# Decode attention over a 65536-row cache on one core: the programs of ACT, SP and GpSimd run the steady heads as loops

## The chip, the core and the metric

The kernel runs on one core of one Trainium2 chip. The core has a matrix engine (PE, with its weight loads shown as PEld), a vector engine (DVE), a scalar engine (ACT), GpSimd (POOL) and a synchronizing engine (SP) that here issues nearly all DMAs. Every engine runs a program of its own; the programs meet only at semaphores. Sixteen DMA engines carry data between HBM and the on-chip memory. The metric is device time in microseconds (us), as the median of several runs. Before the change it is 2518.57 us over three runs (2518.57 to 2519.21).

## The reference

One token of a decode step goes through two branches that a gate mixes: attention over a long cache and a small gated feed-forward.

```python
# x [1,1,512]; k_cache, v_cache [1,32,65536,128]; wq [512,4096]; wo [4096,512]
def _A_ref(x, k_cache, v_cache, wq, wo):
    B, Sq, D = x.shape
    H, Dh = 32, 128
    q = (lambda x, *d: x.transpose(*d))((x @ wq).reshape(B, Sq, H, Dh), 0, 2, 1, 3)
    scores = jnp.einsum("bhqd,bhkd->bhqk", q, k_cache) * (Dh ** -0.5)
    p = _softmax(scores, axis=-1)
    o = jnp.einsum("bhqk,bhkd->bhqd", p, v_cache)
    return (lambda x, *d: x.transpose(*d))(o, 0, 2, 1, 3).reshape(B, Sq, H * Dh) @ wo

def _B_ref(x, w_gate, w_up, w_down):   # 512 -> 1792 -> 512
    g = _silu(x @ w_gate)
    u = x @ w_up
    return (g * u) @ w_down

x = A_x
g = _sigmoid((x * gate_w).sum(-1, keepdims=True))
a = _A_ref(x, A_k_cache, A_v_cache, A_wq, A_wo)
b = _B_ref(x, B_w_gate, B_w_up, B_w_down)
return g * a + (1 - g) * b
```

Inputs are bf16. K and V of one head are 16.78 MB each, and both caches together 1073.7 MB, every byte of which is read once.

## The kernel before

A head's K (65536 rows of 128) is read in two halves of 8.39 MB, z = 0 and 1, and so is its V. A half lies in the on-chip memory as 128 partitions with 64 KB each, taken from 256 consecutive cache rows. The array `mem` is one pool in which these halves have fixed places: `KA` and `KZ` for the K halves, `VA` and `VZ` for the V halves; the places of V overlap those of K and of each other in part, which is why a load has to wait until particular pieces of the half before have been used. Weights and the tail of the last head use the same pool.

For every head DVE transposes K in 16 pieces, 8 of each half (`nc.vector.transpose`, lines 405 and 412; line 336 for head 0), each adding 1 to `ktdone`, into the two buffers of `kt`. PE multiplies each piece with the head's query `qcur` (line 462) and adds 1 to `qkdone`. After the 16th piece DVE takes the row maximum (line 350, `s_mx`). POOL takes the maximum over partitions (`partition_all_reduce`, line 280, `s_ar`), ACT scales it (line 305), computes the exponentials and their row sums in one activation (line 307, `expdone`) and copies the next head's query from `qd` to `qcur` (line 310, `s_qc`). POOL sums the row sums over partitions (line 282, `s_L`). DVE rearranges the exponentials into `pb` in two halves (line 345, `s_pba`, `s_pbz`). PE then multiplies them with V (line 515), four groups of matmuls a head, each of which adds 1 to `pvdone`; these run one head late, between the score matmuls of the next head. ACT normalizes the resulting row (`row_norm`, line 299, `s_or`), PE turns it into a column (line 489, `s_pt`) and ACT puts that column into `oTn` (line 301).

The order of work on each engine is written out by hand. PE runs the 32 heads in a hardware loop (`Fori`, line 494) with further loops inside it, and DVE runs heads 1 to 31 in one (line 393). The programs of SP, POOL and ACT are written out head by head by Python loops: SP at lines 226 to 238, POOL at 278 to 282, ACT at 303 to 312. In these the limits of waits and all addresses are constants, and a wait is carried by the instruction that follows it.

SP's order for one head h is: first K half of h, first V half of h - 1, second K half of h, second V half of h - 1. Each has a wait ahead of it: K waits on `ktdone` (pieces transposed out of the place that it overwrites), V on `pvdone` (value matmuls done). All go to one queue and are carried out in the order of issue. Head 1 has other limits than the rest. After the last head, SP loads the output weights `wo` and the last head's V in pieces of falling size (lines 239 to 250). PE ends with the sums over these pieces (line 544) and the projection (lines 559 and 583), ACT rounds the result (line 314), and SP and ACT store it.

Of the kernel before, what the change touches and what calls it, by code (L numbers as in the profile page):

```python
# [5 lines left out]
P = 128  # L6
# [9 lines left out]
ds = bass.DynSlice  # L16
# [5 lines left out]
def bass_gated_mix__mha_block_cached__swiglu_ffn__decode_kernel(  # L22
# [11 lines left out]
    out: bass.AP,  # L34
):
    _, H, S, Dh = A_k_cache.shape
    D = A_wq.shape[0]
    F = B_w_gate.shape[1]
# [4 lines left out]
    NP = HR // PR  # L43
# [5 lines left out]
    KA, KZ, VA, VZ, V0 = 32, 0, 120, 96, 96  # L49
# [15 lines left out]
    with ExitStack() as ctx:  # L65
        def sb(name, shape, dt):
            return ctx.enter_context(nc.sbuf_tensor(name, shape, dt))

        def psum(name, shape, dt):
            return ctx.enter_context(nc.psum_tensor(name, shape, dt))  # L70

        def sem(name):
            return ctx.enter_context(nc.semaphore(name))
# [6 lines left out]
        psT = psum("psT", [P, 512], F32)  # L80
# [5 lines left out]
        qd = sb("qd", [P, H, 4, 4], BF16)  # L86
        qcur = sb("qcur", [P, 4, 4], BF16)
# [8 lines left out]
        gcol = sb("gcol", [P, 2], F32)  # L96
# [5 lines left out]
        oTn = sb("oTn", [P, H], BF16)  # L102
# [6 lines left out]
        def at(kb, n):  # L109
            return mem[:, kb * KB:kb * KB + n]  # L110
# [9 lines left out]
        d = {n: sem("d_" + n) for n in names}  # L120
# [21 lines left out]
        s_qc = sem("s_qc")  # L142
# [3 lines left out]
        s_b = sem("s_b")  # L146
        s_dch = sem("s_dch")
        ktdone = sem("ktdone")
        qkdone = sem("qkdone")
        pvdone = sem("pvdone")  # L150
        s_mx = sem("s_mx")
        s_ar = sem("s_ar")
        s_nb = sem("s_nb")
        expdone = sem("expdone")
        s_pba = sem("s_pba")
# [5 lines left out]
        s_otn = sem("s_otn")  # L161
# [34 lines left out]

        def place(kind, h, z):
            if kind == "k":
                return (KA, V0)[z] if h == 0 else (KA, KZ)[z]
            return (VA, VZ)[z]  # L200

        def kv_dram(cache, h):
            return cache[0, h].rearrange("(b p r) d -> b p (r d)", b=2, p=P)

        for n, kb in (("wq", WQ), ("wg", WG), ("wu", WU), ("wd", WD)):
            src = w_dram[n]
# [7 lines left out]
        @block.sync  # L214
        def _(sp):
            def load(kind, h, z):
                cache = A_k_cache if kind == "k" else A_v_cache
                sp.dma_start(at(place(kind, h, z), HR * Dh), kv_dram(cache, h)[z]).then_inc(d[kind + "az"[z]], 16)

            half = HR // 2 * Dh  # L220
            for n in range(2):
                sp.dma_start(at(KA + 32 * n, half), kv_dram(A_k_cache, 0)[0][:, n * half:n * half + half]).then_inc(
                    (d["ka0"], d["ka"])[n], 16)
            sp.wait_ge(s_q, 1)
            load("k", 0, 1)
            for h in range(1, H):
                sp.wait_ge(ktdone, 2 * NP * h - 4 if h > 1 else NP)
                load("k", h, 0)
                if h == 1:
                    sp.wait_ge(ktdone, 2 * NP - 3)  # L230
                    sp.wait_ge(s_b, 1)
                else:
                    sp.wait_ge(pvdone, 4 * h - 1)
                load("v", h - 1, 0)
                sp.wait_ge(ktdone, 2 * NP * h + NP // 2)
                load("k", h, 1)
                sp.wait_ge(pvdone, 4 * h + 1)
                load("v", h - 1, 1)
            sp.wait_ge(ktdone, 2 * NP * H - NP)
            sp.dma_start(at(WO, 31 * D), w_dram["wo"][:, 0:31 * D]).then_inc(d["wo"], 16)  # L240
            src = A_v_cache[0, H - 1].rearrange("(b p r) d -> b p (r d)", b=2, p=P)
            need = {0: (ktdone, 2 * NP * H - 4), 1: (ktdone, 2 * NP * H), 2: (pvdone, 4 * H - 1)}
            for n, (kb, r0, nr) in enumerate(tail):
                if n in need:
                    sp.wait_ge(*need[n])
                b, o = divmod(r0, HR)
                sp.dma_start(at(kb, nr * Dh), src[b][:, o * Dh:(o + nr) * Dh]).then_inc(dt_[n], 16)  # L247
            sp.wait_ge(pvdone, 4 * H)
            sp.dma_start(at(WOJ, D), wj_dram).then_inc(d["wj"], 16)
            sp.dma_start(at(WO31, D), w31_dram).then_inc(d["w31"], 16)  # L250
            sp.wait_ge(s_fin, 1)
            sp.dma_start(out_dram[2:4, :], fin[32:34, :]).then_inc(s_out2, 16)

        @block.gpsimd
        def _(pool):
            nc.gpsimd.memset(onesf[0:1, :], 1.0)
            nc.gpsimd.memset(sel, 0.0).then_inc(s_sel0, 1)
            pool.wait_ge(s_sel0, 1)
            for je in range(4):
                off = 64 * (je // 2) + je % 2  # L260
                v = sel[:, je, :].rearrange("p (g d) -> p g d", g=4)
                last = nc.gpsimd.affine_select(out=v, in_=v, compare_op=ALU.not_equal, fill=1.0, base=-off,
                                               pattern=[[0, 4], [-2, 32]], channel_multiplier=1)
            last.then_inc(s_sel, 1)
            nc.gpsimd.memset(unit[:], 0.0).then_inc(s_unit0, 1)
            pool.wait_ge(s_unit0, 1)
            nc.gpsimd.affine_select(out=unit[:], in_=unit[:], compare_op=ALU.not_equal, fill=1.0, base=0,
                                    pattern=[[-1, 4]], channel_multiplier=1).then_inc(s_unit, 1)
            nc.gpsimd.memset(bmat[:], 0.0).then_inc(s_b0, 1)
            for q in range(4):  # L270
                pool.wait_ge(s_b0, q + 1)
                nc.gpsimd.affine_select(out=bmat[:], in_=bmat[:], compare_op=ALU.not_equal, fill=1.0, base=-32 * q,
                                        pattern=[[-1, 32]], channel_multiplier=1).then_inc(s_b0, 1)
            nc.gpsimd.memset(hot[0:1, :, :], 0.0).then_inc(s_hot0, 1)
            pool.wait_ge(s_hot0, 1)
            nc.gpsimd.affine_select(out=hot[0:1, :, :], in_=hot[0:1, :, :], compare_op=ALU.not_equal, fill=1.0,
                                    base=0, pattern=[[1, 2], [-1, 2]], channel_multiplier=0).then_inc(s_hot, 1)
            for h in range(H):
                pool.wait_ge(s_mx, h + 1)
                nc.gpsimd.partition_all_reduce(amx, mxs, P, RMAX).then_inc(s_ar, 1)  # L280
                pool.wait_ge(expdone, h + 1)
                nc.gpsimd.partition_all_reduce(Lt, rsum, P, RADD).then_inc(s_L, 1)  # L282

        @block.scalar
        def _(act):
            act.wait_ge(s_z, 1)
            nc.scalar.activation(sc[0:1, 1:2], sc[0:1, 0:1], ACT.Exp, scale=-1.0).then_inc(s_e1, 1)
            act.wait_ge(s_qd, 1)
            nc.scalar.copy(qcur[:], qd[:, 0, :, :]).then_inc(s_qc, 1)
            act.wait_ge(s_gp, 1)  # L290
            nc.scalar.copy(gcol[:], psM[:, 8:10]).then_inc(s_gc, 1)
            act.wait_ge(s_h, 1)
            nc.scalar.activation(hbuf[:, 0, 0:FC], psM[:, 64:64 + FC], ACT.Exp, scale=-1.0).then_inc(s_sig, 1)

            def row_norm(h):
                act.wait_ge(s_li, h + 1)
                act.wait_ge(pvdone, 4 * h + 8)
                act.wait_ge(s_pt, h + 1)
                nc.scalar.mul(orow[0:4, :], psO[0:4, :], Li[0:4, :]).then_inc(s_or, 1)  # L299
                act.wait_ge(s_pt, h + 2)  # L300
                nc.scalar.mul(oTn[:, h:h + 1], psT[:, 0:1], gcol[:, 0:1]).then_inc(s_otn, 1)  # L301

            for h in range(H):
                act.wait_ge(s_ar, h + 1)
                nc.scalar.mul(nbias, amx, -SCALE).then_inc(s_nb, 1)  # L305
                act.wait_ge(s_nb, h + 1)
                nc.scalar.activation(pa[:], psS[:], ACT.Exp, bias=nbias, scale=SCALE,  # L307
                                     accum_out=rsum).then_inc(expdone, 1)
                if h < H - 1:
                    nc.scalar.copy(qcur[:], qd[:, h + 1, :, :]).then_inc(s_qc, 1)  # L310
                if h >= 1:
                    row_norm(h - 1)
            act.wait_ge(s_z4, 1)
            nc.scalar.copy(fin[0:34, :], psZ[0:34, 0:128]).then_inc(s_fin, 1)  # L314
            act.wait_ge(s_fin, 1)
            act.dma_start(out_dram[0:2, :], fin[0:2, :]).then_inc(s_out, 16)
# [297 lines left out]
```

## Time and profile before

| what | value |
|---|---|
| median of three runs | 2518.57 us |
| the profiled execution, whole | 2518.66 us |
| its span | 2517.4 us |
| mean granted clock of PE | 0.711 of full speed |
| instructions in the trace | 50622 |
| read from HBM | 1087.77 MB, 432 GB/s over the span |
| busy: PE, DVE, ACT, POOL | 1675.3, 1397.7, 65.6, 26.8 us |

The span is the time from the first to the last instruction of the profiled execution; 1.26 us of that execution's time lie around it. The page of the profile cuts the span into 40 slices. A row of the form "SPq" is an instruction of the engine's own sequencer, such as the issue of a DMA, a branch or an operation on registers; such rows are not counted as busy time. A row of waits names the engine and line that waited, what ended the wait, the total, how many times, and the longest. The time from a DMA's issue to its landing includes the time that it spends behind earlier DMAs.

### The profile page before, as it was taken

Reading aid. Unit: us, or ns where it says so; the run is one execution under the profiler, and the core shown is the slowest. Engines: PE = TensorE matmul, PEld = TensorE weight load, DVE = VectorE, ACT = ScalarE, POOL = GpSimd, SP = SyncE. Lnnn points to the kernel's source line nnn. Section 1 sums busy time; section 2 is a strip of 40 time slices with the busy share of each in tenths; the row PEclk is TensorE's granted clock in tenths of the full one; section 3 lists DMA queues with packets and bytes.
Section 4 is the critical chain, followed back from the end, with each engine's and each line's share of the span. In section 5 each row is a group of like instructions: output and inputs, shape, how many; then the busy total and the mean of one; then the engine's idle time right before and its main releaser. Section 6 shows DMA issues by size and latency. Waiting matters only on the chain.

```text
span 2517.4 us, 50622 instructions
## 1 busy us (share of the span) xinstructions
PE 1675.3 (67%) x21432; PEld 956.8 (38%) x21432; DVE 1397.7 (56%) x1631; ACT 65.6 (3%) x195; POOL 26.8 (1%) x83
## 2 busy tenths in 40 slices
PE   4566756667666577566676666766657756667667
PEld 3333333333433334333333333343333433333334
DVE  3764565554655645646456555465464564644653
ACT  0000000000000000000000000000000000000000
POOL 0000000000000000000000000000000000000000
PEclk8667767677677677676776767767767767677677
DMA  9999999999999999999999999999999999999999
GB/s 418 433 433 434 435 433 433 434 433 433 433 433 433 433 433 433 433 433 433 433 435 432 434 433 434 433 434 433 434 433 433 433 433 434 433 433 433 433 434 396
DMA packets 20474, 1087.97 MB, mean 432 GB/s; under 512 B 2282, under 2 KB 2668, under 8 KB 2924
## 3 DMA queue, kind: packets, MB, share of 16 engines
q1 hardware_dynamic: 20452, 1087.78, 99.9%
q8 instruction: 9, 0.15, 0.0%
q14 instruction: 5, 0.04, 0.0%
q10 hardware_dynamic: 8, 0.00, 0.0%
HBM read 1087.77 MB, written 0.00 MB: 432 GB/s over the span
## 4 chain that ended last, share of the span: by engine, by line
DMA 72%; PE 27%; DVE 0%; issue 0%; SPq 0%; ACT 0%
DMA mem<-in_A_v_cache_dram 70%; PE psO L515 27%; DMA mem<-in_A_k_cache_dram 2%; DMA mem<-in_A_wq_dram 1%; DVE kt L336 0%; PE psM L446 0%; SPq L247 0%; PE psZ L583 0%; PE psW L544 0%; ACT fin L314 0%
## 5 line engine op out<-in xcount | busy, mean ns | idle before, releaser
L462 PE MATMUL psS<-qcur,kt 128*128 128x4 bf16 x16384 | 573.7, 169 | 776.4 <-DVE kt L405 458.4
L515 PE MATMUL psO<-mem,pb 128*4 128x512 bf16 x3968 | 1033.6, 428 | 35.2 <-DMA mem<-in_A_v_cache_dram 35.2
L405 DVE STREAM_TRANSPOSE kt<-mem 128x2048 uint32<-128x2048 uint32 x248 | 551.2, 2280 | 571.9 <-DMA mem<-in_A_k_cache_dram 571.0
L462 PEld LDWEIGHTS psS<-qcur,kt 128*128 128x128 bf16 x16384 | 534.7, 106 | 852.4 <-issue 850.0
L412 DVE STREAM_TRANSPOSE kt<-mem 128x2048 uint32<-128x2048 uint32 x248 | 547.6, 2274 | 407.6 <-DMA mem<-in_A_k_cache_dram 407.6
L515 PEld LDWEIGHTS psO<-mem,pb 128*4 128x4 bf16 x3968 | 361.2, 93 | 666.2 <-issue 235.7
L345 DVE COPY pb<-pa 32x64 bf16<-32x64 bf16 x1024 | 233.5, 228 | 24.2 <-PE psO L515 9.5
L350 DVE TENSOR_REDUCE sm<-psS 128x1 f32<-128x512 f32 x32 | 22.1, 692 | 42.3 <-PE psS L462 42.3
L336 DVE STREAM_TRANSPOSE kt<-mem 128x2048 uint32<-128x2048 uint32 x16 | 35.4, 2277 | 16.9 <-DMA mem<-in_A_k_cache_dram 16.9
L280 POOL PARTITION_ALL_REDUCE sm<-sm x32 | 11.2, 351 | 2392.6 <-DVE sm L350 2392.6
L301 ACT ACTIVATE oTn<-psT,gcol 128x1 bf16<-128x1 f32 x31 | 8.2, 263 | 1063.2 <-PE psT L489 1063.2
L489 PE MATMUL psT<-unit,orow 4*128 4x1 f32 x256 | 33.5, 248 | 0.8 <-ACT orow L299 0.8
L299 ACT ACTIVATE orow<-psO,sm 4x512 f32<-4x512 f32 x31 | 21.0, 677 | 439.5 <-issue 439.5
L489 PEld LDWEIGHTS psT<-unit,orow 4*128 4x128 f32 x256 | 30.8, 186 | 1.9 <-ACT orow L299 1.3
L305 ACT ACTIVATE sm<-sm 128x1 f32<-128x1 f32 x32 | 6.5, 203 | 886.3 <-POOL sm L280 886.3
L307 ACT ACTIVATE pa<-psS,sm 128x512 bf16<-128x512 f32 x32 | 22.0, 687 | 1.0
L544 PE MATMUL psW<-pb,mem 128*128 128x1 bf16 x512 | 14.6, 165 | 7.6 <-DMA mem<-in_A_v_cache_dram 7.1
L544 PEld LDWEIGHTS psW<-pb,mem 128*128 128x128 bf16 x512 | 14.1, 102 | 8.7 <-issue 6.5
L282 POOL PARTITION_ALL_REDUCE sm<-sm x32 | 12.3, 383 | 36.4 <-ACT pa L307 36.4
L446 PE MATMUL psM<-xTb,mem 128*128 128x1 bf16 x128 | 3.6, 165 | 11.1 <-DMA mem<-in_A_wq_dram 11.1
L474 PE MATMUL psM<-xTb,mem 128*128 128x1 bf16 x112 | 6.9, 198 | 4.9 <-DMA mem<-in_B_w_up_dram 4.9
L432 DVE TENSOR_SCALAR w<-psW,sm 128x2 bf16<-128x2 f32 x1 | 0.2, 221 | 16.5 <-PE psW L544 16.5
(64 smaller groups left out, 63.1 us busy)
## 6 DMA issues: line engine op xcount, KB each, us to landing
mem<-in_A_v_cache_dram SPq DMA_DIRECT2D x3, 4096.0 KB, 29.4
mem<-in_A_k_cache_dram SPq DMA_DIRECT2D x2, 4096.0 KB, 38.8
mem<-in_A_wq_dram SPq DMA_DIRECT2D x1, 4096.0 KB, 12.6
mem<-in_A_wo_dram SPq DMA_DIRECT2D x1, 3968.0 KB, 37.0
mem<-in_A_v_cache_dram SPq DMA_DIRECT2D x1, 2048.0 KB, 32.9
mem<-in_B_w_gate_dram SPq DMA_DIRECT2D x1, 1792.0 KB, 16.4
mem<-in_B_w_up_dram SPq DMA_DIRECT2D x1, 1792.0 KB, 21.3
mem<-in_B_w_down_dram SPq DMA_DIRECT2D x1, 1792.0 KB, 25.1
```

Of the source, the lines that this page charges most:

```text
L282: nc.gpsimd.partition_all_reduce(Lt, rsum, P, RADD).then_inc(s_L, 1)
L299: nc.scalar.mul(orow[0:4, :], psO[0:4, :], Li[0:4, :]).then_inc(s_or, 1)
L307: nc.scalar.activation(pa[:], psS[:], ACT.Exp, bias=nbias, scale=SCALE, accum_out=rsum).then_inc(expdone, 1)
L336: nc.vector.transpose(kt[:, i % 2, :].rearrange("p (j r t) -> p r j t", j=2, t=32), src.rearrange("p (r j t) -> p r j t", j=2, t=32)).then ...
L345: last = nc.vector.tensor_copy(dst, sr)
L350: nc.vector.reduce_max(mxs, psS[:], AX_X).then_inc(s_mx, 1)
L405: nc.vector.transpose(kt[:, c % 2, :].rearrange("p (j r t) -> p r j t", j=2, t=32), src.rearrange("p (r j t) -> p r j t", j=2, t=32)).then ...
L412: nc.vector.transpose(kt[:, c % 2, :].rearrange("p (j r t) -> p r j t", j=2, t=32), src.rearrange("p (r j t) -> p r j t", j=2, t=32)).then ...
L462: last = nc.tensor.matmul(psS[:, o:o + 4] if j is None else psS[:, ds(j * (2 * PR) + o, 4)], ktb[b][:, je // 2, r, :, je % 2], qcur[:, je, ...
L489: last = nc.tensor.matmul(psT[:, 0:1], orow[0:4, i * Dh:(i + 1) * Dh], unit[0:4, i:i + 1], start=(i == 0), stop=(i == 3))
L515: last = nc.tensor.matmul(psO[0:4, :], pb[:, k_col[256 * z + r]:k_col[256 * z + r] + 4], vt[:, r * Dh:(r + 4) * Dh], start=(z == 0 and par ...
L544: last = nc.tensor.matmul(psW[:, 0:1], vt[:, r * Dh:(r + 1) * Dh], pb[:, col:col + 1], start=(r0 + r == 0), stop=(r0 + r == R - 1))
```

## The change

The steady heads of three engines become hardware loops, each with a counter in a register. Limits of waits and addresses that depend on the head are computed from that counter.

- SP: heads 0 and 1 of K and head 0 of V stay written out. Then a loop of 30 passes issues four loads per pass; the DRAM address comes from the counter (`ds(h, 1)` selects one head of the cache) and the place in `mem` is constant.
- POOL: one loop of 32 passes holds both all-reduces. Between each wait and its all-reduce stands an increment of a new semaphore, `s_pool`, on which nothing waits.
- ACT: the first `exps` and copy of `qcur` and the last `exps` and `row_norm` are written out; the 30 passes between them are a loop with the same order of operations. The copy reads `qd` and the second multiplication writes `oTn` at an address from a register.

PE's and DVE's programs are not touched, and neither is the number of loads, their sizes, their order, or the values that the waits compare with.

```diff
@@ -196,11 +197,13 @@
         def place(kind, h, z):
             if kind == "k":
-                return (KA, V0)[z] if h == 0 else (KA, KZ)[z]
+                return (KA, V0)[z] if isinstance(h, int) and h == 0 else (KA, KZ)[z]
             return (VA, VZ)[z]
 
         def kv_dram(cache, h):
-            return cache[0, h].rearrange("(b p r) d -> b p (r d)", b=2, p=P)
+            if isinstance(h, int):
+                return cache[0, h].rearrange("(b p r) d -> b p (r d)", b=2, p=P)
+            return cache[0, ds(h, 1)].rearrange("a (b p r) d -> b (a p) (r d)", b=2, p=P)
@@ -223,19 +226,24 @@
             load("k", 0, 1)
-            for h in range(1, H):
-                sp.wait_ge(ktdone, 2 * NP * h - 4 if h > 1 else NP)
-                load("k", h, 0)
-                if h == 1:
-                    sp.wait_ge(ktdone, 2 * NP - 3)
-                    sp.wait_ge(s_b, 1)
-                else:
-                    sp.wait_ge(pvdone, 4 * h - 1)
-                load("v", h - 1, 0)
-                sp.wait_ge(ktdone, 2 * NP * h + NP // 2)
-                load("k", h, 1)
-                sp.wait_ge(pvdone, 4 * h + 1)
-                load("v", h - 1, 1)
+            sp.wait_ge(ktdone, NP)
+            load("k", 1, 0)
+            sp.wait_ge(ktdone, 2 * NP - 3)
+            sp.wait_ge(s_b, 1)
+            load("v", 0, 0)
+            sp.wait_ge(ktdone, 2 * NP + NP // 2)
+            load("k", 1, 1)
+            sp.wait_ge(pvdone, 5)
+            load("v", 0, 1)
+            with nc.sync.Fori(0, H - 2) as i:
+                sp.wait_ge(ktdone, i * (2 * NP) + (4 * NP - 4))
+                load("k", i + 2, 0)
+                sp.wait_ge(pvdone, i * 4 + 7)
+                load("v", i + 1, 0)
+                sp.wait_ge(ktdone, i * (2 * NP) + (4 * NP + NP // 2))
+                load("k", i + 2, 1)
+                sp.wait_ge(pvdone, i * 4 + 9)
+                load("v", i + 1, 1)
             sp.wait_ge(ktdone, 2 * NP * H - NP)
@@ -275,10 +283,12 @@
-            for h in range(H):
+            with nc.gpsimd.Fori(0, H) as h:
                 pool.wait_ge(s_mx, h + 1)
+                nc.gpsimd.sem_inc(s_pool, 1)
                 nc.gpsimd.partition_all_reduce(amx, mxs, P, RMAX).then_inc(s_ar, 1)
                 pool.wait_ge(expdone, h + 1)
+                nc.gpsimd.sem_inc(s_pool, 1)
                 nc.gpsimd.partition_all_reduce(Lt, rsum, P, RADD).then_inc(s_L, 1)
@@ -294,22 +304,27 @@
             def row_norm(h):
                 act.wait_ge(s_li, h + 1)
-                act.wait_ge(pvdone, 4 * h + 8)
+                act.wait_ge(pvdone, h * 4 + 8)
                 act.wait_ge(s_pt, h + 1)
                 nc.scalar.mul(orow[0:4, :], psO[0:4, :], Li[0:4, :]).then_inc(s_or, 1)
                 act.wait_ge(s_pt, h + 2)
-                nc.scalar.mul(oTn[:, h:h + 1], psT[:, 0:1], gcol[:, 0:1]).then_inc(s_otn, 1)
-
-            for h in range(H):
+                nc.scalar.mul(oTn[:, ds(h, 1)], psT[:, 0:1], gcol[:, 0:1]).then_inc(s_otn, 1)
+
+            def exps(h):
                 act.wait_ge(s_ar, h + 1)
                 nc.scalar.mul(nbias, amx, -SCALE).then_inc(s_nb, 1)
                 act.wait_ge(s_nb, h + 1)
                 nc.scalar.activation(pa[:], psS[:], ACT.Exp, bias=nbias, scale=SCALE,
                                      accum_out=rsum).then_inc(expdone, 1)
-                if h < H - 1:
-                    nc.scalar.copy(qcur[:], qd[:, h + 1, :, :]).then_inc(s_qc, 1)
-                if h >= 1:
-                    row_norm(h - 1)
+
+            exps(0)
+            nc.scalar.copy(qcur[:], qd[:, 1, :, :]).then_inc(s_qc, 1)
+            with nc.scalar.Fori(0, H - 2) as i:
+                exps(i + 1)
+                nc.scalar.copy(qcur[:], qd[:, ds(i + 2, 1), :, :].rearrange("p a e g -> p (a e) g")).then_inc(s_qc, 1)
+                row_norm(i)
+            exps(H - 1)
+            row_norm(H - 2)
             act.wait_ge(s_z4, 1)
```

## The prediction

> **What bounds the kernel now.** I read the page's table of slices first. Its columns are 40 equal stretches of the span; the digits of DMA are the busy share of the 16 DMA engines, in tenths.
>
> ```profile
> span 2517.4 us, 50622 instructions
> ...
> PE 1675.3 (67%) x21432; PEld 956.8 (38%) x21432; DVE 1397.7 (56%) x1631; ACT 65.6 (3%) x195; POOL 26.8 (1%) x83
> ...
> DMA  9999999999999999999999999999999999999999
> GB/s 418 433 433 434 435 433 433 434 433 433 433 433 433 433 433 433 433 433 433 433 435 432 434 433 434 433 434 433 434 433 433 433 433 434 433 433 433 433 434 396
> ...
> q1 hardware_dynamic: 20452, 1087.78, 99.9%
> q8 instruction: 9, 0.15, 0.0%
> q14 instruction: 5, 0.04, 0.0%
> ```
>
> The DMA engines are full in every slice and carry 433 GB/s in all but the first and the last. 1087.78 MB at that rate is 2512 us of the 2517.4. PE (67%) and DVE (56%) have room; ACT and POOL, two of the three engines whose programs change, are busy 3% and 1%. So the question is only whether the change can leave the DMA engines without queued work, give them more to do, or take something from them. The two "instruction" rows are the engines' own code being fetched over the same DMA engines: 14 packets in the run.
>
> Next the list of DMA issues and of SP's own waits, for how early each load is issued. In the issue line the last number is the median time from issue to landing; the second line is for all loads of source line 218; the others say whom SP waits for.
>
> ```profile
> mem<-in_A_k_cache_dram SPq DMA_DIRECT2D x63, 29.7
> mem<-in_A_v_cache_dram SPq DMA_DIRECT2D x62, 27.8
> ```
> ```profile
> DMA to landing us min/median/max: 26.9/29.6/48.9
> ```
> ```profile
> SPq L218 <- PE psO L515: 1277.0, 61, 21.8
> SPq L218 <- DVE kt L405: 528.9, 31, 17.9
> SPq L218 <- DVE kt L412: 513.1, 30, 17.9
> ```
> ```profile
> 1991.04 0.33 SPq L218 DMA_DIRECT2D mem<-in_A_k_cache_dram  x1
> 2011.82 0.33 SPq L218 DMA_DIRECT2D mem<-in_A_v_cache_dram  x1
> 2029.74 0.33 SPq L218 DMA_DIRECT2D mem<-in_A_k_cache_dram  x1
> 2051.79 0.33 SPq L218 DMA_DIRECT2D mem<-in_A_v_cache_dram  x1
> 2068.73 0.33 SPq L218 DMA_DIRECT2D mem<-in_A_k_cache_dram  x1
> ```
>
> SP issues one 8.39 MB load (half of a head's K or V), then sits in the next wait for 17 to 21 us (1277.0/61 for V, 528.9/31 for K). K issues are 38.70 us apart (1991.04 to 2029.74), two loads in that time, so one load occupies the engines for 19.35 us (433.5 GB/s). The fastest one landed 26.9 us after its issue, so at the worst issue of the run 26.9 - 19.35 = 7.55 us of earlier work was still queued; at a median K issue 10.3 us. That 7.55 us is the cover of everything SP does in its loop. The chain of waits on the page (72% V and K loads, 27% the 40 value matmuls that let the next V load be issued) looks like a loop through PE, but by this backlog a later issue only shortens the time its load stands in the queue; it does not move the landing.
>
> **The change part by part.** All sums are against the profiled execution, 2518.66 us (span 2517.4 and 1.26 around it), 0.09 us above the median of 2518.57.
>
> *SP's loop, 30 passes of 4 loads.* Today a wait rides on the DMA instruction itself, which takes 0.33 us. With register addresses and limits, register instructions stand ahead of it. DVE and PE already run such loops, and their rows price them: ALU_OP 40 ns on DVE, FUSED_REGOPS 46 ns on PE, two consecutive ones on DVE start 0.11 us apart. What computes the limit runs before the wait and lies in SP's 17 to 21 us of waiting. What computes the address can stand between the wait and the DMA: an estimate of 3 such instructions by 0.11, and 0.10 because a DMA whose wait is not on it took 0.43 us (the tail's row, 0.33 to 0.43): 0.43 us per issue. Bounds: 0.1 us (one instruction) and 1.5 us (ten instructions, 1.1, with 0.10 and the back edge). I take 0.43, nearest to DVE's loop, which puts one to three in front of an instruction. The back edge: DVE's COMPARE_BRANCH took 56 ns at the median and its next instruction began 0.29 us after it; PE's took 209 ns. It falls once per pass, after a V issue, ahead of a wait of 17 us. All of this is below 7.55 us, so it costs 0. Were the cover gone, 120 issues by 0.43 would be 52 us. Leaving the loop delays the issue of the WO load at 2438.52 by some 0.4 us; it stood 37.0 us until landing, behind a V load, so 0.
>
> *POOL's loop, 32 passes, with two increments of s_pool each.* Nobody waits for s_pool. POOL sits between the row maximum and the exponential: reduce, POOL (0.35), ACT's scaling (0.20), exponential (0.69), then qcur for the next head's scores. Two increments, two limits and a back edge add about 0.1 + 0.1 us ahead of each all-reduce (EVENT_SEMAPHORE rows: 17 to 51 ns; register instructions as above); bounds 0 and 0.6. At a steady head qcur is ready at 1229.23 and PE first needs it at 1249.15, because K lands only at 1246.7: 17 us and more of cover. At head 0 to 1 the cover is thin: qcur ends at 87.4, the first transposed K at 87.9. If POOL costs over 0.5 us there, PE's scores are late, then DVE's transposes, then the K load issued at 94.52; but the V load before that lands at 104.8, 10.3 us later. In the last head the exponential ends near 2468, DVE's rearrangement at 2472, and its first reader on PE begins at 2485.32, waiting for a V load: 13 us. Cost 0 in all three.
>
> *ACT's loop, 30 passes.* Some ten register instructions a pass (limits of six waits, two addresses, the counter), about 1 us, spread over 77 us of which ACT is busy 2. qcur has the 17 us above; the normalized row is written at 1244.27 and PE waits for it ahead of the value matmuls at 1265.97, which wait for V anyway: 21 us. What follows the loop (exponential of head 31 at 2467.2) has 26 us after the last instruction of the loop. Cost 0.
>
> *What is removed: code fetches.* The written-out programs do not fit in what is fetched at the start; the five packets on q14 are 8 KB each. Four of them fall deep in the steady heads (613.7, 628.2, 1377.2 and 2022.3 us), the fifth at 96.2. Each took 0.31 to 0.32 us on one DMA engine, and the 64 KB packet beside it took 2.77 to 2.84 us in place of 2.42. Whether that reaches the end depends on whether that engine is the one that finishes last. SP's own cadence shows it: the K interval after 2029.74 is 38.99 against 38.70, +0.29 after the fetch at 2022.3; across the other three it stays at 38.70 or 38.71. So removal gains 0.3 us; bounds 0 and 4 x 0.38 = 1.5 us.
>
> Here a rule speaks against the change. Back edges first, as the trace has them:
>
> ```profile
> L393 DVEq COMPARE_BRANCH  x31: 50/56/67, 143.3 to 2465.9; - x31
> ```
> ```profile
> L528 PEldq COMPARE_BRANCH  x32: 67/68/3137, 56.0 to 2439.2; - x32
> ```
>
> (min, median, max in ns.) DVE jumped back 30 times through a body of 70 instructions, never over 67 ns, and q14 shows five fetches in all. One branch on PE, on its first pass at 56.0, took 3137 ns, with a 16 KB fetch on q8 inside it: that is the price of a target that is not there. The Trainium skill, Runtime: NRT & Kernel Launch, section Instruction fetch mechanics, says that only two blocks of code are held, that prefetch is sequential, and that a taken branch out of that window waits for a fetch by DMA. By that, a loop astride two blocks could refetch at every pass; the 3137 ns agrees with the rule, the 31 quick passes of DVE show that a loop of that length need not pay it.
>
> **Sum:** 2518.66 + 0 (SP) + 0 (POOL) + 0 (ACT) - 0.3 (fetches) - 0.09 to the median = 2518.3 us. Its own range, 2516.8 to 2519.9: down by 1.5, up by 1.6 for small shifts at start and end, where the runs before already spread by 0.64.
>
> **Rivals.**
> 1. *A back edge that refetches (slower).* One new loop loses its block on every pass. The stall of 3.1 us is still under 7.55 us, so SP's lateness is hidden; what costs is the DMA time: 30 fetches by 0.38 us on one engine, 11.4 us if that is the engine that ends last: 2529.7. For it: the 3137 ns branch. Against: DVE and PE, 31 and 32 passes with longer bodies than any new one (some 20 to 30 instructions) and 14 fetches in the run. It decides from 14 refetching passes on the last engine (5 us). Chance 0.05.
> 2. *Loads by register are cut into smaller packets (slower).* The 64 KB packets run at 432.9 GB/s (2.422 us each), the 32 KB packets of the first and last loads at 431.9 (1.214). Halved everywhere, 2512 us grow by 0.25%: 2524.5. The new view of the cache has one more axis, of length one, which is what could do it; each row is contiguous as before, which speaks against it. Chance 0.03.
> 3. *SP's issue is later than the backlog lasts (slower).* It needs over 7.55 us per issue, five times my upper bound; each microsecond over costs up to 62 us (62 V loads). 2580 at one over. Chance 0.01.
> 4. *Fetches mattered more than the cadence shows (faster).* All four on the pacing engine: 2517.1. That is still within 0.2%. To gain 5 us something of the 433 GB/s itself would have to change, for which no row speaks: chance 0.03.
>
> **How the numbers follow.** 0.2% is 5.0 us, about what a measurement of this kernel can tell from no change: same is 2513.5 to 2523.6. The forecast with the near half of rival 4 has 0.88; rivals 1 to 3 sum to 0.09, slower; 0.03 faster. The range for 8 in 10 is the forecast's own, widened to 2516.0 and 2521.0 for end effects that no row prices; the far rivals stay outside with their 0.12.
>
> **What the profile would show.** Right: 433 GB/s in all middle slices, K issues 38.70 us apart, q14 with fewer than five packets, landing times of V shorter by SP's new delay (27.8 to about 27.4), new SPq, ACTq and POOLq rows of ALU_OP and COMPARE_BRANCH. Rival 1: q14 with 30 packets or more and branches of about 3 us. Rival 2: near twice the 20474 packets. Rival 3: landing times near 19.4 us and slices under 433. The forecast is wrong if the interval of 38.70 changes.

## The result, and the profile after

| | before | after |
|---|---|---|
| time, median (lowest to highest), 22 runs each | 2518.88 us (2518.55 to 2519.37) | 2522.52 us (2521.08 to 2524.80) |
| the profiled execution | 2518.66 us, span 2517.4 | 2521.97 us, span 2520.7 |
| GpSimd's first all-reduce begins | 85.84 us | 94.85 us |
| q14 code fetches | 5 | 1 |

The changed kernel is slower: 1.0014 of the time before, 95% interval 1.0008 to 1.0021. That is 3.64 us, below the 0.2% that I called a measurable difference, yet above the 2521.0 at which my range ended, and the two sets of times don't overlap. The changed kernel's times also spread more: 3.7 us from lowest to highest, against 0.8.

The page of the changed kernel has the same shape as the one before; what differs stands in the first slices and in the last.

```profile
span 2520.7 us, 51479 instructions
...
GB/s 418 419 432 433 434 433 433 433 433 434 434 438 438 434 433 433 433 433 434 434 433 433 433 434 433 433 433 433 434 436 434 435 436 435 434 433 433 433 434 389
...
q1 hardware_dynamic: 20452, 1087.78, 99.9%
...
q14 instruction: 1, 0.01, 0.0%
```

The second slice (63 to 126 us) moves 419 GB/s where it moved 433, and the slices after it, up to the last, move 432 to 438. So most of the loss is taken at the start. The timelines of SP's loads around that point show it too (start in us, duration, instruction), before first, then after:

```profile
77.11 0.33 SPq L218 DMA_DIRECT2D mem<-in_A_v_cache_dram  x1
94.52 0.33 SPq L218 DMA_DIRECT2D mem<-in_A_k_cache_dram  x1
116.33 0.33 SPq L218 DMA_DIRECT2D mem<-in_A_v_cache_dram  x1
```
```profile
77.13 0.33 SPq L221 DMA_DIRECT2D mem<-in_A_v_cache_dram  x1
102.39 0.33 SPq L221 DMA_DIRECT2D mem<-in_A_k_cache_dram  x1
122.60 0.33 SPq L221 DMA_DIRECT2D mem<-in_A_v_cache_dram  x1
...
1994.83 0.33 SPq L221 DMA_DIRECT2D mem<-in_A_k_cache_dram  x1
...
2033.51 0.33 SPq L221 DMA_DIRECT2D mem<-in_A_k_cache_dram  x1
```

The load at 77.1 is level. The next, the second half of head 1's K, is issued 7.87 us late, the V load after it 6.27 us late. At 1994.83 the lag is 3.79 us (1991.04 before), and from there to the next K issue it is 38.68 us, the interval before (38.70). Nothing is lost in the steady heads; something is lost once, and stays.

What made that K load late is found by going back along its waits. Timeline of before, head 0 to head 1 (in brackets the idle time ahead of the instruction and what ended it):

```profile
85.01 0.69 DVE L350 TENSOR_REDUCE sm<-psS 128x1 f32<-128x512 f32 x1 [1.35 <-PE psS L462]
...
85.84 0.38 POOL L280 PARTITION_ALL_REDUCE sm<-sm  x1 [69.78 <-DVE sm L350]
...
87.16 0.19 ACT L310 COPY qcur<-qd 128x16 bf16<-128x16 bf16 x1
...
88.06 1.15 PE L462 MATMUL psS<-qcur,kt 128*128 128x4 bf16 x32 [3.09 <-DVE kt L405]
```

The same of after:

```profile
85.02 0.69 DVE L365 TENSOR_REDUCE sm<-psS 128x1 f32<-128x512 f32 x1 [1.34 <-PE psS L477]
...
94.85 0.38 POOL L289 PARTITION_ALL_REDUCE sm<-sm  x1 [77.96 <-issue]
...
96.17 0.19 ACT L321 COPY qcur<-qd 128x16 bf16<-128x16 bf16 x1
...
96.67 2.32 PE L477 MATMUL psS<-qcur,kt 128*128 128x4 bf16 x64 [11.69 <-ACT qcur L321]
...
97.86 4.50 DVE L420 STREAM_TRANSPOSE kt<-mem 128x2048 uint32<-128x2048 uint32 x2 [7.74 <-PE psS L477]
```

The row maximum ends at 85.7 us in both. Before, GpSimd's all-reduce begins 0.1 us later; after, 9.1 us later. ACT's copy to `qcur`, PE's scores, DVE's transposes and with them SP's K load follow. PE now waits 11.69 us for `qcur`; before it waited 3.09 us for the transposed K. The idle time on GpSimd is no longer put down to DVE but to "issue", that is, to nothing that the profile can name. The rows of GpSimd's sequencer name it. Line view of before, then of after (durations in ns min/median/max, then the times at which the first and last began; an indented line is the idle time ahead of an engine's instructions, with what ended it, and how often):

```profile
L280 POOL PARTITION_ALL_REDUCE sm<-sm x32: 350/350/381, 85.8 to 2466.6; - x32
L280 POOLq MODIFY_POOL_CONFIG  x2: 1/1/1, 16.3 to 16.3; - x2
```
```profile
L289 POOLq MODIFY_POOL_CONFIG  x64: 11/11/11, 86.1 to 2470.1; - x64
L289 POOL PARTITION_ALL_REDUCE sm<-sm x32: 350/350/375, 94.9 to 2470.2; - x32
...
  issue: 78.0, 1
```

Two `MODIFY_POOL_CONFIG` stand in GpSimd's program ahead of the first all-reduce, where it goes over from `affine_select`. Before, nothing stood in front of them: the wait for `s_mx` rode on the all-reduce itself. They ran at 16.3 us, and the all-reduce of 85.8 came without a stall. After, the wait rides on the new `sem_inc`, an instruction of its own, and the two stand behind it: they run at 86.1 us, once the row maximum is there, and the all-reduce follows 8.7 us later. No packet of q14 falls into this time: the only one starts at 103.7 us. In the other 31 passes they take 11 ns each, and the all-reduce begins within 0.1 us of the second.

What this did to the DMA engines, in a table by stretches, before first (columns: stretch in us, its length, busy time and instructions of PE, PEld, DVE, ACT, POOL, granted clock, DMA share, GB/s):

```profile
100.00:106.00 6.00, 3.52 (x67) 2.55 (x68) 6.00 (x4) 0.00 (x0) 0.00 (x0) 0.50 1.04 448
106.00:120.00 14.00, 14.00 (x116) 6.58 (x115) 4.93 (x18) 0.00 (x0) 0.00 (x0) 0.85 1.01 435
120.00:126.00 6.00, 4.23 (x20) 1.50 (x18) 1.74 (x1) 0.00 (x0) 0.00 (x0) 1.00 1.01 437
126.00:180.00 54.00, 31.18 (x480) 19.83 (x480) 33.40 (x31) 1.75 (x5) 0.73 (x2) 0.67 1.00 433
```
```profile
100.00:106.00 6.00, 2.36 (x64) 2.20 (x64) 5.79 (x18) 0.00 (x0) 0.00 (x0) 0.50 0.88 340
106.00:120.00 14.00, 10.06 (x93) 4.98 (x94) 12.76 (x22) 0.00 (x0) 0.00 (x0) 0.67 1.03 445
120.00:126.00 6.00, 6.00 (x87) 3.78 (x86) 0.00 (x0) 0.00 (x0) 0.00 (x0) 0.96 0.92 350
126.00:180.00 54.00, 35.95 (x470) 20.36 (x468) 31.92 (x30) 1.75 (x5) 0.73 (x2) 0.69 0.99 427
```

The engines run partly dry twice, once behind each late issue: 340 for 448 GB/s, and 350 for 437. The view counts a packet whole in the stretch in which it starts, so its differences are rough. From the packets' records, with the bytes of each spread over its own time, the changed kernel is 1.1 us behind at 110 us, 2.3 us at 130 and 2.4 us at 2300; the rest of the 3.3 us by which the span grew is added by the last loads (below).

### The profile page after: what moved, and what is told of

It is laid out like the page before. It is cut to its first block, busy times and chain, and to the rows that moved or that the text cites. A ratio compares the mean times of both kernels' runs of the same rounds, so it can differ in the third digit from the quotient of the medians.

```text
span 2520.7 us, 51479 instructions
## 1 busy us (share of the span) xinstructions
PE 1678.4 (67%) x21432; PEld 956.9 (38%) x21432; DVE 1397.5 (55%) x1631; ACT 65.6 (3%) x195; POOL 26.8 (1%) x83
## 3 DMA queue, kind: packets, MB, share of 16 engines
q1 hardware_dynamic: 20452, 1087.78, 99.9%
## 4 chain that ended last, share of the span: by engine, by line
DMA 69%; PE 28%; DVE 1%; issue 1%; SPq 0%; ACT 0%; POOL 0%; DVEq 0%; ACTq 0%; POOLq 0%
DMA mem<-in_A_v_cache_dram 66%; PE psO L530 27%; DMA mem<-in_A_k_cache_dram 2%; DMA mem<-in_A_wo_dram 1%; DVE kt L351 1%; DMA mem<-in_A_wq_dram 1%; DVE kt L427 0%; PE psS L477 0%; DVE kt L420 0%; SPq L221 0%; PE psM L461 0%; DVE pb L360 0%; PE psT L504 0%; DVE sm L365 0%; PE psZ L598 0%
## 5 line engine op out<-in xcount | busy, mean ns | idle before, releaser
L360 DVE COPY pb<-pa 32x64 bf16<-32x64 bf16 x1024 | 233.1, 228 | 25.1 <-PE psO L530 10.2
L311 ACT ACTIVATE oTn<-psT,gcol 128x1 f32 (+1 forms) x31 | 8.2, 264 | 1069.9 <-PE psT L504 1069.9
L574 PE MATMUL psY<-mem,oR 128*1 128x512 bf16 x31 | 9.5, 480 | 0.3 <-DVE oR L441 0.3
## 6 DMA issues: line engine op xcount, KB each, us to landing
mem<-in_A_wq_dram SPq DMA_DIRECT2D x1, 4096.0 KB, 13.1
```

The costliest lines, as they stand in the source:

```text
L360: last = nc.vector.tensor_copy(dst, sr)
```

## The experiments

Two theories at first. The one in the readings above: the switch ahead of GpSimd's first all-reduce, put behind the wait by the increment, is the whole loss (A). Against it: the loops of SP and ACT, with their register instructions and back edges, cost the 3.6 us, and the late all-reduce is covered as I had argued (B). Then, once A stood: how much lateness is covered, and by what. Times are medians; ratios are to the kernel before, with 95% intervals. All kernels below compute everything; some do extra work, which is named.

**1. SP's and ACT's loops without GpSimd's** (from the changed kernel).

```diff
-            with nc.gpsimd.Fori(0, H) as h:
+            for h in range(H):
                 pool.wait_ge(s_mx, h + 1)
-                nc.gpsimd.sem_inc(s_pool, 1)
                 nc.gpsimd.partition_all_reduce(amx, mxs, P, RMAX).then_inc(s_ar, 1)
                 pool.wait_ge(expdone, h + 1)
-                nc.gpsimd.sem_inc(s_pool, 1)
```

> SP and ACT run loops as in the changed kernel; POOL's program is written out as before. Theory A (the changed kernel loses its time once, in POOL's first all-reduce, which starts 8.7 us later after the row maximum because the two MODIFY_POOL_CONFIG that stand ahead of it now run only after the wait): those configurations are back at 16.3 us, the first all-reduce follows the row maximum within 0.2 us, the second half of K of head 1 is issued near 94.5 us, and the time is that of before less what the missing code fetches give, 2518.6 to 2519.0 us. Theory B (SP's register instructions between wait and DMA, 0.3 us per issue, cost the time by way of the queue): nothing changes against the changed kernel, 2522.5 us, and the K issue near 102 us stays only if POOL is its cause.

Measured: 2518.64 us (2518.44 to 2519.00), 0.9999 (0.999 to 1.0008). The line view of its all-reduce and SP's timeline:

```profile
L288 POOLq MODIFY_POOL_CONFIG  x2: 1/1/1, 17.8 to 17.9; - x2
```
```profile
95.02 0.33 SPq L221 DMA_DIRECT2D mem<-in_A_k_cache_dram  x1
```

With GpSimd written out the two configurations are back ahead of the wait, at 17.8 us, the K load is at 95.02, and the loss is gone. The loops of SP and ACT cost nothing that shows.

**2. GpSimd's loop alone** (from the kernel before: the loop and the two increments, nothing else).

```diff
-            for h in range(H):
+            with nc.gpsimd.Fori(0, H) as h:
                 pool.wait_ge(s_mx, h + 1)
+                nc.gpsimd.sem_inc(s_pool, 1)
                 nc.gpsimd.partition_all_reduce(amx, mxs, P, RMAX).then_inc(s_ar, 1)
                 pool.wait_ge(expdone, h + 1)
+                nc.gpsimd.sem_inc(s_pool, 1)
```

> Only POOL runs its loop with the two increments; SP and ACT are written out as before. Theory A: the stall of 8.7 us ahead of the first all-reduce is there, the K issue comes near 102.4 us, bytes lag by 2.2 to 2.6 us from 130 us on, and the time is 2522 to 2523 us, up to 0.3 above the changed kernel because SP's and ACT's code fetches are back. Theory B: the time of before, 2518.9 us.

Measured: 2522.82 us (2521.87 to 2525.42), 1.0016 (1.0007 to 1.0026). All of the loss is in GpSimd's part. In the profiled execution, by the line view, the stall was longer, 10.6 us:

```profile
L282 POOLq MODIFY_POOL_CONFIG  x64: 11/11/11, 86.1 to 2471.5; - x64
L282 POOL PARTITION_ALL_REDUCE sm<-sm x32: 350/351/377, 96.8 to 2471.6; - x32
```

The K load went out at 104.30.

**3. All three loops, with the switch made early** (from the changed kernel: one all-reduce over a spare column ahead of GpSimd's loop).

```diff
+            nc.gpsimd.memset(sm[:, 7:8], 0.0).then_inc(s_warm, 1)
+            pool.wait_ge(s_warm, 1)
+            nc.gpsimd.partition_all_reduce(wred[:], sm[:, 7:8], P, RMAX).then_inc(s_warm, 1)
             with nc.gpsimd.Fori(0, H) as h:
```

> The changed kernel, with one all-reduce over a spare column ahead of POOL's loop, so that POOL's switch to that operation happens before 30 us. Theory A: the stall goes to that place, where POOL idles; passes of the loop show none; the time is 2518.6 to 2518.9 us, 0 to 0.3 below the kernel before (four code fetches less). Theory C (each pass of POOL's loop is slow, not the first alone, or the configurations inside the loop stall at every pass): the time stays near 2522.5 us.

Measured: 2518.62 us (2518.53 to 2519.13), 0.9999 (0.999 to 1.0008). The line views of the spare all-reduce and of the loop's:

```profile
L290 POOLq MODIFY_POOL_CONFIG  x2: 1/1/1, 16.6 to 16.7; - x2
L290 POOL PARTITION_ALL_REDUCE wred<-sm x1: 377/377/377, 26.8 to 26.8; - x1
...
  issue: 10.4, 1
```
```profile
L294 POOL PARTITION_ALL_REDUCE sm<-sm x32: 350/351/353, 86.1 to 2466.5; - x32
```

The stall is still there, 10.1 us from the configuration at 16.7 to the spare all-reduce at 26.8, but GpSimd has nothing else to do then. The loop's first all-reduce begins at 86.1 and the loss is gone, with loop, increments and back edges all in place. Only the configurations have gone from the loop: its line has no such row any more. This is the version to keep of those with loops: level with the kernel before.

**4. One increment, no loop** (from the kernel before).

```diff
             for h in range(H):
                 pool.wait_ge(s_mx, h + 1)
+                if h == 0:
+                    nc.gpsimd.sem_inc(s_pool, 1)
                 nc.gpsimd.partition_all_reduce(amx, mxs, P, RMAX).then_inc(s_ar, 1)
```

> The kernel before, all written out, with a single increment of a semaphore put between the first wait on the row maximum and the first all-reduce. Theory A: the increment takes the wait, the configurations of the all-reduce fall behind it, and the whole loss appears without any loop: 2522 to 2523 us, the first all-reduce 8.7 us late. Theory D (the loop itself, its entry or its back edge, makes POOL late): the time of before, 2518.9 us.

Measured: 2522.39 us (2521.12 to 2525.18), 1.0015 (1.0006 to 1.0024). Its line view:

```profile
L283 POOL PARTITION_ALL_REDUCE sm<-sm x32: 350/351/377, 97.3 to 2471.2; - x32
L283 POOLq MODIFY_POOL_CONFIG  x2: 11/11/11, 86.4 to 86.5; - x2
```

A single instruction that takes the wait away from the all-reduce brings the whole loss, 3.5 us. No loop, register or back edge is needed. The stall is 10.8 us here. Experiments 1 to 4 settle A against B.

**5 and 6. How late may GpSimd be?** From the kernel before, the first pass is delayed by spare all-reduces, 14 of them (4.6 us by their row) and 40 (13.1 us). The wait rides on the first of these, so the configurations run ahead of it (16.6 and 17.3 us). Two readings: only what exceeds a cover is lost (A1), or a fixed share of the lateness reaches the end (A2).

```diff
                 pool.wait_ge(s_mx, h + 1)
+                if h == 0:
+                    for _ in range(14):      # 40 in the second kernel
+                        nc.gpsimd.partition_all_reduce(wred[:, _:_ + 1], sm[:, 7:8], P, RMAX)
```

> The kernel before, all written out, with 14 all-reduces over a spare column, some 5 us of work, between the first row maximum and its all-reduce; POOL's switch to that operation stays ahead. Theory A1 (a delay of head 0 costs only what it exceeds the queued work by: V's first half lands on the first DMA engine 2 us before the last one, and a load starts 1 us after its issue, so 10.3 - 2.0 - 1.0 = 7.3 us of cover): cost 0, 2518.9 us, K issued near 99.5 us, no lag of bytes. Theory A2 (the delay costs in proportion, 3.5 us for 8.7): 2520.9 us.

> The same with 40 all-reduces over the spare column, some 14 us. Theory A1: the first gap is 14 - 7.3 = 6 to 7 us long, a second one of about 1 us follows at the next V load, 2525 to 2527 us. Theory A2: 14 / 8.7 x 3.5 = 5.6 us, 2524.5 us.

Measured: 2518.84 us (2518.64 to 2519.33), 1.0000 (0.9991 to 1.001) with 14, and 2525.92 us (2525.44 to 2526.77), 1.0029 (1.0018 to 1.0039) with 40. Timeline of the second, then its first stretch in the columns used above:

```profile
86.17 13.07 POOL L286 PARTITION_ALL_REDUCE wred<-sm  x40 [69.08 <-DVE sm L357]
```
```profile
100.00:106.00 6.00, 3.51 (x96) 3.27 (x96) 3.79 (x2) 0.71 (x3) 0.39 (x1) 0.50 0.41 176
```

The DMA engines fall to 176 GB/s there. Put in one table with the other profiled executions, by how much later than before each issue came (94.52 and 116.33), and how much longer the span was (2517.4):

| kernel | K load issued late by | V load issued late by | span longer by |
|---|---|---|---|
| 14 spare all-reduces | 3.58 us | 3.31 us | 0.5 us |
| changed kernel | 7.87 | 6.27 | 3.3 |
| GpSimd's loop alone | 9.78 | 9.32 | 4.9 |
| one increment | 10.30 | 8.86 | 4.6 |
| 40 spare all-reduces | 12.22 | 10.89 | 6.9 |

A lateness of 3.58 us left the median where it was; of 7.87 us and more, all but 4.6 to 5.7 us shows in the span: A1. From the K load alone (the times at which equal numbers of bytes had arrived, compared with before, from the packets' records, at 110 us): 0.01, 1.12, 2.79, 3.22 and 5.30 us were lost by its gap, down the table. From 7.87 on that is its lateness less 6.8 to 7.1 us. So that is the cover at this issue, where I had 10.3. The rest is lost at the V load and in the spread of the engines (below).

**7. SP late at every V load** (from kernel 3: an empty inner loop of 17 passes between the wait and the load of each steady V issue). It tests the 7.55 us that I called the cover of everything that SP does.

```diff
                 sp.wait_ge(pvdone, i * 4 + 7)      # and at + 9
+                nc.sync.sem_inc(s_spin, 1)
+                with nc.sync.Fori(0, 17):
+                    sp.wait_ge(s_q, 1)
                 load("v", i + 1, 0)
```

> The kernel with the early first all-reduce, and in SP's loop 17 empty inner passes, some 6 us, between the wait of each V load and its issue (60 loads). If the cover of a steady V load is 7.55 us, as the prediction had it from the last landing: 2518.6 us. Theory A1 (less 2 us of spread between engines and 1 us from issue to first packet, so 4.5 us): each V load leaves a gap of 1 to 1.5 us, 2580 to 2610 us, with fewer than 433 GB/s in all slices.

Measured: 2544.05 us (2531.65 to 2551.98, 4 runs), 1.0100 (1.0062 to 1.0139). The DMA view, then the page's line on packets:

```profile
mem<-in_A_v_cache_dram SPq DMA_DIRECT2D x62, 23.7
```
```profile
DMA packets 20470, 1087.93 MB, mean 429 GB/s; under 512 B 2282, under 2 KB 2668, under 8 KB 2924
```

The delay came out smaller than meant: a pass takes 0.25 us, so 17 passes make 4.3 us, 4.5 at most, and not 6; the size expected for 6 us is missed for that reason. But the sign decides: by a cover of 7.55 us a delay of 4.5 us would have been free, and it cost 25.4 us against kernel 3 in the median (13 to 33 us in the four runs), 0.42 us at each of 60 V loads (25.4 / 60). The median from issue to landing of a V load fell from 27.6 in kernel 3 to 23.7 us, and below 433 GB/s were moved. The cover of a steady V issue is thus about 4 us, an estimate (4.3 to 4.5 less 0.42).

**8 to 10. What a back edge out of the fetched code would cost** (the first rival). From kernel 3, GpSimd's body is made long. In kernel 8 each pass also writes 520 single elements with memsets, behind the second all-reduce, so the body has over 520 instructions.

```diff
                 nc.gpsimd.partition_all_reduce(Lt, rsum, P, RADD).then_inc(s_L, 1)
+                pool.wait_ge(s_L, h + 1)
+                nc.gpsimd.sem_inc(s_pool, 1)
+                for _ in range(520):
+                    last = nc.gpsimd.memset(wl[32 * (_ % 4):32 * (_ % 4) + 1, _ // 4:_ // 4 + 1], 0.0)
+                last.then_inc(s_long, 1)
+                pool.wait_ge(s_long, h + 2)
+                nc.gpsimd.sem_inc(s_pool, 1)
```

> The kernel with the early first all-reduce, and 520 one-element memsets in each pass of POOL's loop, where POOL idles 75 us; the body is then over 33 KB of code. Theory F (a back edge out of the code that is held refetches it): four or five fetches of 8 KB per pass on q14, 130 to 160 in the run, each taking about 0.3 us of one DMA engine; if they spread over the engines, 130 x 0.31 / 16 = 3 us, 2521 to 2522 us; if all fall on the engine that finishes last, up to 50 us more. Theory G (code that has run once stays): q14 with under ten packets, 2518.6 us.

Measured: 2662.37 us (2661.84 to 2664.03), 1.0571 (1.0553 to 1.0589). That is far above what either reading had. It mixes two things, the code fetched and GpSimd's own work, so each was tried alone: kernel 9 has 520 increments of spare semaphores in the place of the memsets (`for m in range(520): nc.gpsimd.sem_inc(s_fill[m % 16], 1)`), kernel 10 the 520 memsets in a short body:

```diff
+                with nc.gpsimd.Fori(0, 13) as j:
+                    for m in range(40):
+                        last = nc.gpsimd.memset(wl[32 * (m % 4):32 * (m % 4) + 1, m // 4:m // 4 + 1], 0.0)
+                    last.then_inc(s_long, 1)
+                    pool.wait_ge(s_long, h * 13 + j + 2)
+                    nc.gpsimd.sem_inc(s_pool, 1)
```

> The long body of POOL's loop took 2662.4 us with 191 fetches on q14; this run keeps the code length and drops the memory writes: 520 increments of spare semaphores per pass in place of the 520 memsets. Theory F (the fetches cost the time, 143.5 / 190 = 0.76 us each, because they all fall on the one DMA engine that then finishes last): q14 near 190 packets, 2650 to 2665 us. Theory M (the memsets disturb the loads or make POOL late): q14 near 190 packets, yet under 2530 us.

> The counterpart: the same 520 one-element memsets per pass, as 13 turns of an inner loop with 40 memsets, so that the body stays under 80 instructions. Theory F: q14 with one packet, 2518.6 us. Theory M: 2650 us or more with no fetches.

Measured: 2644.13 us (2643.65 to 2644.79), 1.0497 (1.0479 to 1.0514) for 9, and 2558.59 us (2555.30 to 2561.12), 1.0153 (1.0136 to 1.0170) for 10. From the page of 9, and the timeline of the end of 10:

```profile
DMA packets 20660, 1089.49 MB, mean 412 GB/s; under 512 B 2282, under 2 KB 2668, under 8 KB 2924
...
q14 instruction: 191, 1.56, 0.1%
```
```profile
2518.15 0.33 SPq L264 DMA_DIRECT2D out_dram<-fin  x1
...
2553.45 5.21 POOL L305 MEMSET wl<- 1x1 bf16 x40 [0.50 <-POOL wl L305]
```

Kernel 9 fetches six 8 KB packets of code a pass, 191 in all, and runs at 412 GB/s. GpSimd is not late in it: in the view of waits it waits 2501.4 us for DVE. So the 126.3 us (span 2643.5 against kernel 3's 2517.2) are the price of 190 fetches, 0.66 us each; the time lies just below the 2650 to 2665 us that were expected. The packets show what makes up the 0.66: the fetch at 184.66 us takes 0.31 us, and the 64 KB packet that begins right behind it takes 2.77 us in place of 2.42. That leaves nothing for the 520 increments themselves, which were not run in a short body.

Kernel 10 fetches two packets in all and moves 428 to 438 GB/s in the steady slices. SP issues the store of the result at 2518.15 us, 2.1 us later than before (2516.04); from there to the end of the span, 41 us, GpSimd alone still works, on the spare memsets of the last pass. Nearly all of what kernel 10 costs is thus this remainder, which neither reading had expected. Kernel 8 ends in the same way: its store is issued at 2642.24 us, kernel 9's at 2642.19, and the 18.8 us from there to the end of its span are such memsets. So its loss is the fetches' and, behind the store, the memsets'.

## Why the prediction was wrong

*What failed: the step "POOL's loop".* I priced two increments, two limits and a back edge at 0.1 + 0.1 us ahead of each all-reduce, with bounds 0 and 0.6. At head 0 to 1 it was 9.0 us (94.85 less 85.84). The instructions that were added cost what I said: in the other 31 passes the all-reduce begins 0.27 us after the row maximum, where it was 0.09 before. What I didn't ask is which instruction would carry the wait afterwards, and what stood between it and the all-reduce. The trace of before held two rows for that, neither of which I used: the configurations at 16.3 us, which belong to an all-reduce that begins 69.5 us later, and, in the view of waits, the first operation on GpSimd:

```profile
POOL mem L262 <- issue: 11.3, 1, 11.3
```
```profile
L262 POOLq MODIFY_POOL_CONFIG  x2: 11/11/11, 1.6 to 1.6; - x2
```

That is the first `affine_select`, ahead of which GpSimd stood idle for 11.3 us with nothing to wait for, behind two configurations of the same name (the second row, from the line view). The nearest row for the cost of going over to another kind of operation was thus 11.3 us, and bounds of 0 and 11.3 would have put the step beside the cover at head 0 to 1, where it belonged. The Trainium skill, GPSIMD Engine Reference, section 2.1 Instruction dispatch, has this rule too: the first call after such a configuration pays a load of the operation's code, some 6 us, that no instruction shows. By these traces it is more, 8.7 to 11.0 us for the all-reduce, and by them it comes at the first switch alone; the 62 later configurations of the changed kernel cost 11 ns each.

*What failed next to it: the cover, "10.3 us later".* I named the right place and the right chain: qcur, PE's scores, DVE's transposes, and the K load issued at 94.52. But I measured its cover to 104.84, when PE went on with the load before it. By the packets' records the last packet of that load ended at 104.33, the first of the 16 DMA engines was done with it at 102.28, and a new load's first packet begins about 1.0 us after its issue (102.39 and 103.38 in the changed kernel): 102.28 - 94.52 - 1.0 = 6.8, and the changed kernel and experiments 2, 4 and 6 put it at 6.8 to 7.1. The delay of 7.87 us exceeded it by 1.1. The V load after it then had less queued ahead of it too, and its gap took another 1.2 us. By the packets' times the bytes are 2.3 us behind at 130 to 160 us and 2.36 us at 2300. The last packet of all loads ends 3.33 us later than before (2518.13 against 2514.80), so about another 1.0 us is lost at the end, where the DMA engines finish further apart: 2.95 us from the first to the last in the last steady loads, where it was 2.34. Together that is the 3.3 us of the span. Why the engines stay further apart to the end I can't say; no run separates it.

*The steady cover, "7.55 us of earlier work".* Wrong for the same reason: experiment 7 has about 4. It cost nothing here, since SP's part was far below either.

*SP's loop.* Right. The rows of SP's sequencer after show 0.16 us from the end of the wait to the DMA (0.43 was the estimate, 0.1 and 1.5 the bounds); the DMA itself stayed at 0.33. The row of its register instructions, from the line view:

```profile
L221 SPq FUSED_REGOPS  x120: 37/44/57, 137.7 to 2442.4; - x120
```

The landing time of V loads fell from 27.8 to 27.5 us as forecast (27.4), and experiment 1 shows a cost of 0. ACT's loop too is in that experiment.

*Code fetches.* q14 went from five packets to one. Experiments 1 and 3 lie 0.25 and 0.27 us below the kernel before, against a forecast of 0.3, but their intervals reach to 1.0008, so the size is not settled.

*The rivals.* The back edges are short in all new loops (45 ns at most on SP and ACT, 54 on GpSimd), the packets were not cut (one q14 packet, 20452 on q1 as before), and landing times stayed at 24 us and above. None of the three happened. The first one's price, though, was too low: a fetch cost 0.66 us, not 0.38, where many fall on one DMA engine. The 0.38 counted only how much longer the 64 KB packet behind it took, and left out the 0.31 us of the fetch's own packet, which stood beside it. And the rival that did happen was missing: I had a wait on GpSimd that moves from one instruction to another, and no row of mine for it. The Trainium skill's rule on refetching (Runtime: NRT & Kernel Launch, section Instruction fetch mechanics) agrees with these traces: six fetches a pass for the body of over 520 instructions, none for the short ones.

## What to carry to other kernels

An instruction put between a wait and the operation that used to carry it takes the wait, and what the operation has in front of it (here its configuration, and with it the stall) moves behind the wait. Before pricing such an edit, look in the line view for instructions of that line which ran long ahead of it; where there are any, an early spare call of the operation, where nothing waits, can take the stall out of the way, as in experiment 3. And measure the cover of a DMA to the moment at which the first engine is done with the load before, from the first packet, not from issue to the last landing: here that was about 7 us for 10.3, and about 4 for 7.55.

## What the runs showed of the hardware that I had not expected

The first switch from `affine_select` to the all-reduce on GpSimd held it for 8.7 to 11.0 us in eight profiled executions (8.7 in the changed kernel, 10.6, 10.1 and 10.8 in experiments 2, 3 and 4, 10.1, 11.0, 10.2 and 9.9 in 7 to 10), with no instruction in the trace. It differs from run to run, which fits the wider spread of the kernels that expose it (3.6 to 4.1 us from lowest to highest in experiments 2 and 4 and the changed kernel, 0.6 in 1 and 3), though no run shows the one by the other.

190 code fetches of 8 KB, 1.56 MB of 1089, cost 126 us. The bytes alone would be 3.6 us at 433 GB/s. In kernel 9 fifteen of the 16 DMA engines finish a steady load within 0.8 us, and one finishes 8.5 us behind the first of them (medians; before, all 16 finish within 2.0 us). The late one is the one that fetches: the 64 KB packet right behind the fetch at 184.66 us ends at 187.74, when that last engine ends its load, and the other fifteen ended between 180.4 and 182.4. Followed back packet by packet, the late engine's work leads to a fetch in 73 of 111 steady loads; in the others the records don't tell the engines apart. So the fetches put one engine behind, and every load waits for its last one. Why the four that the kernel before had in its steady heads cost 0.3 us at most no run shows; they need not fall on the engine that is last.
